# Channel attention feeding a gated MLP: seven-product pairs in batches 0 and 3, other tiles for staging and squares, a changed plan

## The chip, the core and the metric

The kernel runs on one core of one Trainium2 chip. The metric is the device time of one execution, in microseconds (us).

## What is computed

For each of B = 4 batches, with N = 6080 tokens and C = 256 channels, all in float32:

```python
qn = q / (norm(q, over tokens) + 1e-6)          # q, k, v: (4, 6080, 256)
kn = k / (norm(k, over tokens) + 1e-6)
s  = kn.T @ qn / tau                            # 256 x 256 channel scores
a  = exp(s - s.max(-1));  a /= a.sum(-1) + 1e-9
x  = v @ a                                      # 24320 tokens x 256 in all
h  = x @ w_in                                   # 256 -> 2048
g  = h * sigmoid(1.702 * h)
out = g @ w_out                                 # 2048 -> 256
```

The weights come as 64-bit floats and are turned into float32 on the chip.

## The kernel before

**Folding.** The kernel never forms x. For each batch it multiplies a with w_in once (`weights`, matmuls at line 689) and then applies that product to v. Tokens lie last, so a chunk is 1024 tokens wide (the sixth of a batch 960), cut into two halves of 512 (480) columns. A batch has six chunks, and a chunk has eight *pairs* (`NPAIR`), each for 256 of the 2048 hidden features. Pairs are numbered through by `place`: eight in a chunk, 48 in a batch.

**Three matmuls for one product.** A float32 operand is split in a rounded high part and the rest (the helper `cast` at line 283 on ScalarE, `low` at line 306 on VectorE). `three` (line 773) multiplies high by high, high by low and low by high: three matmuls make one *product*.

**Seven or eight products.** A pair multiplies 2 x 2 blocks twice. The first time (`front`: weights w by values v, into the PSUM banks X, Y, Z) it always takes seven products by a Strassen-like scheme. Then ScalarE applies the gate (line 799), and the result is the tile ga, the matrix G of the title. The second time (`back`: G by w_out, into the banks O2, O3, O4, O7 and K) it takes eight plain products, or seven. With seven (`is_s`), VectorE first forms sums of blocks of G in the tile gp (three additions: p13 over 1024 columns, p2 and p4 over 512), and casts and rests are made of the tiles gi (1536 columns), gr and gj (1024 each). With eight, only gi and gj of 1024 columns each are made.

**Groups.** `groups_of(b, c)` says for each chunk how its eight pairs are grouped: a tuple (a, z) is a group of a pairs in seven products followed by z in eight. A group uses the one bank K in turn for the sums of M1, M6, M5 (if a > 0) and of plain products (if z > 0); each sum is taken out of K before the next begins (`evac`, tiles ka to kd; ScalarE copies in a chunk's first group, VectorE adds in later ones). The weights of M6 and M5 of a group are in one tile wb, a slot for each pair of seven. Chunk 0 of batch 0 has two groups (0, 4).

**The attention side.** For batches 0 and 1 the scores are made directly from float32 rows of q and k (`load_direct`, then `unit`, matmuls at line 536); for 2 and 3 from parts that POOL's queue casts while loading (line 280, matmuls at line 542). A unit is two tiles of 128 tokens. Beside the scores it squares the rows (ScalarE, line 512 or 519) and adds the squares to acc (VectorE, line 291); the first matmuls of `finish` (line 588) sum acc over partitions for the norms. `finish` goes on with a power on POOL, scaling, the exponentials (line 628) and a dummy gate that loads the gate's table again (line 640). For batch 0 the squares go to the tile wi, for batch 1 to gp, each a single buffer; raw rows come in four tiles gr0, gj0, gr1, gj1 for batch 0 and in gr0, gr1 for batch 1.

**Conversions.** In chunk 0 of batch 0, w_in and w_out are converted piecewise (`win_convert`, `wout_convert`): loaded as words in the raw tile vr (the same as for the values' v_raw), worked on by VectorE, stored to win_d and wout_d, and loaded from there for use. `wout_convert` works in the tile gr2.

**The order.** Nothing is issued directly. `Plan.add` records each step with its engine, a cost in ns, a lag until its result is there, its dependencies, its tiles and a due time. `Plan.order` places all steps on the engines with a list schedule, forward and backward four times over, and keeps the shortest plan; between engines it counts `HOP` ns. The engines then run their steps in that order. Work for a later batch is tied to a place by `todo`: score units of batch 2 to places 19 to 60, of batch 3 to 74 to 118, softmax and weights after them. Each such step depends, for its loads, on `here`, the first product M1 of the pair at its place.

## Time and profile before

| what | value |
| --- | --- |
| runs | 2161.42, 2163.58, 2167.99 us, median 2163.58 |
| the profiled execution's own time | 2159.93 us |
| its span in the trace | 2158.2 us |
| busy: TensorE matmuls, weight loads | 2107.5 us (98%), 1748.2 us (81%) |
| busy: VectorE, ScalarE, GpSimd | 1831.9 us (85%), 1600.6 us (74%), 77.8 us (4%) |
| granted TensorE clock, mean | 0.993 |
| moved by DMA | 513.24 MB, 238 GB/s |

The page gives for each engine its busy time, then groups of instructions by line, tile and shape, with what ended the idle time before them. PE is TensorE's matmuls, PEld its weight loads, DVE VectorE, ACT ScalarE, POOL GpSimd and SP the engine that issues most DMAs. Matmuls overlap, so the duration of one is not its pitch.

### The profile page before, as it was taken

To read this page: it belongs to the slowest core of one execution; us is meant where nothing else is said; L and a number is where in the kernel's file an instruction comes from. 1 tells how busy PE (TensorE), PEld (TensorE's weight loads), DVE (VectorE), ACT (ScalarE), POOL (GpSimd) and SP (SyncE) were. 2 spreads that over 40 slices of the span, in tenths; PEclk is the share of its full clock that TensorE was granted. 3 is DMA by queue.
4 is the path that set the end of the run, shared out by engine and by line. 5 is a ranking of instruction groups with operands and counts; after the bars stand their busy time and mean duration, and the time that the engine had idled before them with its cause. 6 is when DMAs were issued, how large, how long until landed. Compare 5 with 4: busy or idle time off the path is not lost.

```text
span 2158.2 us, 27036 instructions
## 1 busy us (share of the span) xinstructions
PE 2107.5 (98%) x9724; PEld 1748.2 (81%) x9724; DVE 1831.9 (85%) x2295; ACT 1600.6 (74%) x2345; POOL 77.8 (4%) x110
## 2 busy tenths in 40 slices
PE   8698999999999999999999999999999999999999
PEld 7586788888888888878888888878888888888887
DVE  6897877888878889888898898898987978888796
ACT  4575877676777778877777777787777778777775
POOL 0000000000000000000000000000000000000000
PEclk9899999999999999999999999999999999999999
DMA  8897677767677656886776777647856655655553
GB/s 307 276 327 261 244 278 271 241 227 253 216 250 260 212 207 237 324 263 213 260 251 227 243 250 243 214 168 290 299 195 225 225 190 197 223 195 204 205 200 140
DMA packets 204150, 513.24 MB, mean 238 GB/s; under 512 B 16112, under 2 KB 82160, under 8 KB 202992
## 3 DMA queue, kind: packets, MB, share of 16 engines
q1 hardware_dynamic: 178096, 486.60, 64.0%
q0 software_dynamic: 25920, 24.91, 4.8%
q8 instruction: 77, 1.26, 0.2%
q14 instruction: 57, 0.47, 0.1%
HBM read 444.60 MB, written 66.85 MB: 237 GB/s over the span
## 4 chain that ended last, share of the span: by engine, by line
PE 78%; DVE 9%; DMA 6%; issue 3%; ACT 2%; SPq 0%; POOL 0%; POOLq 0%; DVEq 0%; ACTq 0%
PE ps_o L773 24%; PE ps_X L773 15%; PE ps_k L773 13%; PE ps_Y L773 10%; PE ps_Z L773 10%; PE ps_s L542 3%; PE ps_w L689 2%; DVE acc L291 2%; PE ps_s L536 2%; DMA w<-w_d 1%; DMA v_raw<-in_vT 1%; DMA hl<-in_k 1%; DVE gi L306 1%; DVE gp L291 1%; DMA raw<-in_k 1%
## 5 line engine op out<-in xcount | busy, mean ns | idle before, releaser
L773 PE MATMUL ps_X<-v,w 128*128 128x512 f32 (+1 forms) x1728 | 489.6, 392 | 5.7 <-DVE ga L291 1.7
L773 PE MATMUL ps_o<-gi,wo 128*128 128x512 f32 (+1 forms) x1536 | 412.2, 388 | 0.1
L773 PEld LDWEIGHTS ps_X<-v,w 128*128 128x128 f32 x1728 | 320.4, 188 | 80.2 <-ACT ps_Z L283 7.9
L799 ACT ACTIVATE ga<-ga 128x512 f32<-128x512 f32 (+1 forms) x384 | 237.3, 627 | 184.4 <-DVE ga L291 183.2
L306 DVE TENSOR_TENSOR gi<-ga,gi 128x1536 fp32r<-128x1536 f32 (+2 forms) x192 | 299.8, 1561 | 50.9 <-ACT gi L283 46.1
L773 PE MATMUL ps_Z<-v,w 128*128 128x512 f32 (+1 forms) x1152 | 326.4, 391 | 9.0 <-ACT w L283 5.4
L773 PEld LDWEIGHTS ps_o<-gi,wo 128*128 128x128 f32 x1536 | 287.6, 188 | 58.4 <-DVE gi L306 0.5
L773 PE MATMUL ps_Y<-v,w 128*128 128x512 f32 (+1 forms) x1152 | 326.2, 391 | 0.8 <-DVE ga L291 0.6
L773 PE MATMUL ps_o<-gj,wo 128*128 128x512 f32 (+1 forms) x1152 | 310.0, 390 | 1.2 <-DVE gj L306 1.1
L283 ACT CAST gi<-ga 128x1536 fp32r<-128x1536 f32 (+2 forms) x192 | 254.9, 1328 | 20.2 <-PE ps_o L773 14.6
L773 PEld LDWEIGHTS ps_Z<-v,w 128*128 128x128 f32 x1152 | 215.2, 188 | 58.3 <-ACT w L283 6.1
L773 PEld LDWEIGHTS ps_o<-gj,wo 128*128 128x128 f32 x1152 | 215.8, 189 | 45.2 <-DVE gj L306 1.7
L773 PEld LDWEIGHTS ps_Y<-v,w 128*128 128x128 f32 x1152 | 211.2, 188 | 48.3 <-ACT ps_Y L283 4.5
L773 PE MATMUL ps_k<-gr,wb 128*128 128x512 f32 (+1 forms) x768 | 205.0, 388 | 0.0
L291 DVE TENSOR_TENSOR gp<-ga 128x1024 f32<-128x1024 f32 (+1 forms) x128 | 154.9, 1210 | 35.4 <-ACT ga L799 34.3
L306 DVE TENSOR_TENSOR gj<-gp,gj 128x1024 fp32r<-128x1024 f32 (+1 forms) x128 | 154.7, 1209 | 22.1 <-ACT gj L283 21.8
L291 DVE TENSOR_TENSOR ga<-ps_X,m 128x512 f32<-128x512 f32 (+1 forms) x192 | 130.4, 679 | 49.6 <-PE ps_X L773 40.0
L306 DVE TENSOR_TENSOR gr<-gp,gr 128x1024 fp32r<-128x1024 f32 (+1 forms) x128 | 154.6, 1208 | 17.4 <-ACT gr L283 17.4
L773 PEld LDWEIGHTS ps_k<-gr,wb 128*128 128x128 f32 x768 | 143.4, 188 | 29.4 <-ACT ka L283 0.4
L283 ACT CAST gr<-gp 128x1024 fp32r<-128x1024 f32 (+1 forms) x128 | 133.2, 1041 | 28.7 <-DVE gp L291 23.6
L283 ACT COPY ps_Y<-ps_X 128x512 f32<-128x512 f32 (+1 forms) x192 | 110.7, 577 | 54.1 <-PE ps_X L773 52.7
L291 DVE TENSOR_TENSOR ga<-ps_Y,m 128x512 f32<-128x512 f32 (+1 forms) x192 | 130.4, 679 | 22.3 <-PE ps_Y L773 22.3
(119 smaller groups left out, 2834.6 us busy)
## 6 DMA issues: line engine op xcount, KB each, us to landing
w<-w_d SPq DMA_DIRECT2D x184, 896.0 KB, 5.4
wo<-wout_d SPq DMA_DIRECT2D x128, 640.0 KB, 5.8
wo<-wout_d SPq DMA_DIRECT2D x64, 512.0 KB, 5.7
wb<-wout_d SPq DMA_DIRECT2D x128, 256.0 KB, 3.9
w_d<-wst SPq DMA_DIRECT2D x24, 896.0 KB, 5.2
v_raw<-in_vT SPq DMA_DIRECT2D x20, 1024.0 KB, 8.5
out_T<-oc SPq DMA_DIRECT2D x80, 256.0 KB, 5.2
wi<-win_d SPq DMA_DIRECT2D x32, 512.0 KB, 5.3
```

The costliest lines, as they stand in the source:

```text
L283: return g.add("ACT", act(n, psum), lambda: nc.scalar.copy(dst(), src()), deps, uses, due)
L291: return g.add("DVE", dve(n), lambda: nc.vector.tensor_tensor(dst(), a(), b(), op=op), deps, uses, due)
L306: lambda: nc.vector.tensor_tensor(dst(), src(), hi().bitcast(F32), op=ALU.subtract),
L536: nc.tensor.matmul(out, lhsT=buf()[:pp, 1, o + j, ci], rhs=buf()[:pp, 0, o + j, :], start=begin, stop=True, skip_group_check=True,)
L542: nc.tensor.matmul(out, lhsT=hl()[:pp, 1, j, l, ci], rhs=hl()[:pp, 0, j, r, :], start=begin and m == 0, stop=True, skip_group_check=True,)
L689: nc.tensor.matmul(pb()[:, i * 2 * P : (i + 1) * 2 * P], lhsT=at.aT()[:, l, j, ci], rhs=wi()[:, m, j, :], start=i == 0 and n == 0, stop=Tr ...
L773: nc.tensor.matmul(dst, lhsT=l(a), rhs=r(b), start=begin and n == 0, stop=True, skip_group_check=True,)
L799: lambda: nc.scalar.activation(dst(), src(), AF.Gelu_apprx_sigmoid, scale=sign), deps, uses, at,
```

## The change

Batch 0 gets the groups of batches 1 and 2 in its chunks 1 to 5 (six pairs of eight in seven products, before four of eight). Batch 3 gets groups of three, three and two pairs, all in seven products. Raw rows of batch 1 come in four tiles for the first eight loads, then in two. Batch 0's squares go to the weight tiles w0 and w1 in turn, batch 1's are made in place, after the scores that read the tile; batch 1's acc lies in gp instead of wb. `win_convert` loads its words in gr2 instead of vr, and `wout_convert` works in wb instead of gr2. The exponentials and the dummy gate become separate steps. Loads tied to a place depend on M1 of the pair two places before. The plan counts 70 ns for a hop and longer lags for the score loads.

```diff
-    HOP = 40
+    HOP = 70
...
 ONE, TWO, THREE = ((2, 2), (2, 2)), ((3, 1), (3, 1)), ((3, 0), (3, 0), (2, 0))
...
     if b == c == 0:
         return FIRST
-    return (ONE, TWO, TWO, TWO)[b]
+    return (TWO, TWO, TWO, THREE)[b]
...
+AHEAD = 2
+STAGES = ("gr0", "gj0", "gr1", "gj1") * 2 + ("gr0", "gr1") * 4
...
-        return g.add("POOL", 800, lambda: nc.gpsimd.dma_start(dst(), src()), deps, uses, due, lag=6000)
+        return g.add("POOL", 800, lambda: nc.gpsimd.dma_start(dst(), src()), deps, uses, due, lag=8000)
...
-        f = sbuf("gr2", [P, 8, P], F32, "cf")
+        f = sbuf("wb", [P, 8, P], F32, "cf")
...
-            self.acc = sbuf("wb" if b == 1 else "acc", [P, 2, UT, C], F32, "acc")
+            self.acc = sbuf("gp" if b == 1 else "acc", [P, 2, UT, C], F32, "acc")
...
-                        lambda i=i: view(i), lambda i=i: self.rows(i, t0, nt, pp), 128 * nt, after, [t], due - 10, 5000,
+                        lambda i=i: view(i), lambda i=i: self.rows(i, t0, nt, pp), 128 * nt, after, [t], due - 10, 7000,
...
-                sq = sbuf(("wi", "gp")[self.b], [P, 2, UT, C], F32, "sq") if self.direct else buf
-                s = g.add(
-                    "ACT", act(w),
-                    lambda: nc.scalar.activation(sq()[:pp, :, :nt, :], src(), AF.Square), ok, [buf, sq], due + 1,
-                )
...
+                sq = buf if self.b else sbuf(f"w{u % 2}", [P, 2, UT, C], F32, "sq")
+                sqv = (lambda: src()) if self.b else (lambda: sq()[:pp, :, :nt, :])
+                if self.b == 1:
+                    ok = news
+                s = g.add(
+                    "ACT", act(w),
+                    lambda: nc.scalar.activation(sqv(), src(), AF.Square), ok, [buf, sq], due + 1,
+                )
...
-            e = g.add("ACT", 4200, fn_ee, e, [both, mx, zs], due + 0.9)
+            e = [
+                g.add("ACT", 700 + 1300 * (i == 0), lambda i=i: fn_e(i), [e[i]], [both, mx, zs], due + 0.9 + 0.01 * i)
+                for i in range(NC2)
+            ]
+
+            g.add(
+                "ACT", 1500, lambda: nc.scalar.activation(mx(), mx(), AF.Gelu_apprx_sigmoid), e, [mx], due + 0.95,
+            )
...
-        nxt.load_direct(t0, RT, f"gr{slot % 2}", -80.0 + 2.2 * t0)
+        nxt.load_direct(t0, RT, STAGES[slot], -80.0 + 2.2 * t0)
...
+            heres.append(here)
...
-                    win_convert(grp, cc, t + 3 + 3 * cc, "vr", "oc1")
+                    win_convert(grp, cc, t + 3 + 3 * cc, "gr2", "oc1")
...
-                fn(t, here)
+                fn(t, heres[max(0, place - AHEAD)])
```

The blocks that square and add in `unit` also move behind the scores of the unit, in the order in which steps are recorded.

## Rows read from the trace of the kernel before

**Rows 1.** The page's part 1: busy time, share of the span, instructions.
```profile
PE 2107.5 (98%) x9724; PEld 1748.2 (81%) x9724; DVE 1831.9 (85%) x2295; ACT 1600.6 (74%) x2345; POOL 77.8 (4%) x110
```
**Rows 2.** Stretches: from:to, length, each engine's busy time (instructions), granted clock, DMA.
```profile
0.00:75.00 75.00, 55.07 (x263) 47.62 (x264) 53.15 (x78) 37.57 (x43) 1.73 (x7) 0.90 0.85 298
75.00:197.00 122.00, 116.10 (x539) 97.08 (x538) 110.44 (x179) 83.83 (x120) 0.00 (x0) 0.98 0.82 286
197.00:222.00 25.00, 17.93 (x66) 12.89 (x65) 17.99 (x30) 13.28 (x20) 0.00 (x0) 0.80 0.88 323
300.00:700.00 400.00, 397.43 (x1882) 331.84 (x1881) 329.06 (x394) 288.88 (x429) 30.21 (x42) 1.00 0.74 247
700.00:900.00 200.00, 199.53 (x945) 166.20 (x944) 178.38 (x233) 161.01 (x238) 6.04 (x9) 1.00 0.69 242
900.00:1690.00 790.00, 780.13 (x3619) 646.72 (x3618) 697.25 (x847) 604.57 (x890) 38.85 (x51) 1.00 0.70 239
1690.00:2100.00 410.00, 409.87 (x1798) 334.97 (x1798) 342.64 (x401) 314.22 (x465) 0.00 (x0) 1.00 0.59 204
2100.00:2159.00 59.00, 54.24 (x251) 46.42 (x249) 40.78 (x48) 33.85 (x52) 0.00 (x0) 1.00 0.40 143
```
**Rows 3.** Stretches, the same columns: two of the minutes with the busiest VectorE.
```profile
720.00:780.00 60.00, 59.53 (x277) 48.81 (x276) 57.19 (x69) 47.51 (x68) 3.58 (x6) 1.00 0.66 223
1320.00:1380.00 60.00, 58.77 (x274) 48.52 (x274) 56.46 (x67) 46.10 (x66) 3.96 (x6) 1.00 0.67 222
```
**Rows 4.** TensorE's waits, 60 to 120 us: who <- for what, us, times, longest.
```profile
PE ps_n L588 <- DVE acc L291: 13.3, 1, 13.3
PE ps_s L536 <- DMA raw<-in_k: 5.6, 3, 4.0
```
**Rows 5.** The start in order of time: start, us, engine, instruction [idle before].
```profile
18.70 1.06 ACT L519 ACTIVATE sq<-raw 128x1024 f32<-128x1024 f32 x1 [1.29 <-DVE acc L291]
19.79 1.23 DVE L291 TENSOR_TENSOR acc<-acc,sq 128x1024 f32<-128x1024 f32 x1 [1.12 <-ACT sq L519]
...
56.80 1.03 PE L536 MATMUL ps_s<-raw 128*128 128x256 f32 x4
...
71.09 1.84 PE L588 MATMUL ps_n<-ones,acc 128*128 128x1 f32 x8 [13.27 <-DVE acc L291]
```
**Rows 6.** TensorE's waits, 120 to 330 us: the longest line.
```profile
PE ps_Z L773 <- ACT w L283: 5.4, 2, 4.1
```
**Rows 7.** SP's queue in order of time: the load of chunk 1's values.
```profile
201.85 0.38 SPq L276 DMA_DIRECT2D v_raw<-in_vT  x1
```
**Rows 8.** Groups by shape, whole span: count, busy us, mean ns, idle before.
```profile
L306 DVE TENSOR_TENSOR gi<-ga,gi 128x1536 fp32r<-128x1536 f32 x106 | 185.8, 1753 | 30.8 <-ACT gi L283 26.0 <-PE ps_k L773 4.1
L291 DVE TENSOR_TENSOR gp<-ga 128x1024 f32<-128x1024 f32 x106 | 129.5, 1221 | 27.7 <-ACT ga L799 26.9
L306 DVE TENSOR_TENSOR gj<-gp,gj 128x1024 fp32r<-128x1024 f32 x106 | 129.3, 1220 | 17.3 <-ACT gj L283 17.0
L306 DVE TENSOR_TENSOR gr<-gp,gr 128x1024 fp32r<-128x1024 f32 x106 | 129.2, 1219 | 13.2 <-ACT gr L283 13.2
L291 DVE TENSOR_TENSOR gp<-ga,gp 128x512 f32<-128x512 f32 x106 | 72.7, 686 | 4.0 <-ACT ga L799 1.5
...
L297 DVE SCALAR_TENSOR_TENSOR gj<-ga,gj 128x1024 fp32r<-128x1024 f32 x54 | 66.0, 1222 | 21.5 <-ACT gj L858 21.4
L306 DVE TENSOR_TENSOR gi<-ga,gi 128x1024 fp32r<-128x1024 f32 x54 | 66.0, 1221 | 8.2 <-ACT gi L283 8.1
```
**Rows 9.** VectorE in batch 3 in order of time: two neighbours that overlap.
```profile
1805.21 1.75 DVE L306 TENSOR_TENSOR gi<-ga,gi 128x1536 fp32r<-128x1536 f32 x1
1806.88 1.22 DVE L306 TENSOR_TENSOR gj<-gp,gj 128x1024 fp32r<-128x1024 f32 x1
```
**Rows 10.** VectorE at the end in order of time: K's third sum.
```profile
2149.72 0.66 DVE L291 TENSOR_TENSOR kc<-ps_k,kc 128x480 f32<-128x480 f32 x1 [2.88 <-PE ps_k L773]
```
**Rows 11.** ScalarE in the first softmax in order of time: the table load.
```profile
82.69 1.28 ACT L640 ACT_TABLE_LOAD   x1
```

More of the change, by code (lines that the diff above doesn't have):

```diff
@@ L509, in unit @@
                 ok, uses = [l], [hl]
-            if u == 0:
-                self.acc_n = [g.add(
-                    "ACT", act(w), lambda: nc.scalar.activation(acc(), src(), AF.Square), ok, [buf, acc], due + 0.5,
-                )]
-            else:
-                sq = sbuf(("wi", "gp")[self.b], [P, 2, UT, C], F32, "sq") if self.direct else buf
-                s = g.add(
-                    "ACT", act(w),
-                    lambda: nc.scalar.activation(sq()[:pp, :, :nt, :], src(), AF.Square), ok, [buf, sq], due + 1,
-                )
-                a = lambda: acc()[:pp, :, :nt, :]
-                self.acc_n = [tt(
-                    a, a, lambda: sq()[:pp, :, :nt, :], ALU.add, w, [s, *self.acc_n], [sq, acc], due + 1.5,
-                )]
             S = self.S if self.direct else bank("Z", "s")
@@ L552, in unit @@
                 news.append(n)
+            if u == 0:
+                self.acc_n = [g.add(
+                    "ACT", act(w), lambda: nc.scalar.activation(acc(), src(), AF.Square), ok, [buf, acc], due + 0.5,
+                )]
+            else:
+                sq = buf if self.b else sbuf(f"w{u % 2}", [P, 2, UT, C], F32, "sq")
[6 more added lines that the diff above has]
+                )
+                a = lambda: acc()[:pp, :, :nt, :]
+                self.acc_n = [tt(
+                    a, a, sqv, ALU.add, w, [s, *self.acc_n], [sq, acc], due + 1.5,
+                )]
             if self.direct:
@@ L635, in finish @@
             ]
-            def fn_ee():
-                for i in range(NC2):
-                    fn_e(i)
-                nc.scalar.activation(mx(), mx(), AF.Gelu_apprx_sigmoid)
-            e = g.add("ACT", 4200, fn_ee, e, [both, mx, zs], due + 0.9)
+            e = [
[5 more added lines that the diff above has]
+            )
             def fn_z():
@@ L648, in fn_z @@
                     nc.vector.tensor_scalar_mul(x()[:, i, :], x()[:, i, :], zs()[:, i : i + 1])
-            e = g.add("DVE", 1300, fn_z, [e], [both, zs], due + 1)
+            e = g.add("DVE", 1300, fn_z, e, [both, zs], due + 1)
             due = yield
@@ L1094, in channel_attention_then_glu @@
     place = 0
+    heres = []
     for b in range(B):
```

## Prediction

> **What bounds the kernel now.** I read the busy shares first: TensorE is busy for 2107.5 of 2158.2 us [rows 1], so 50.7 us of idle time are all that a better order can win; the rest has to come from less work. Then the table of stretches [rows 2], which splits these 50.7 us: the first 75 us hold 19.9 of them, 75 to 197 us 5.9, the 25 us from 197 on 7.1, the last 59 us under 5. In batch 0 (300 to 700 us) TensorE is idle for 2.6 of 400 us, in batches 1 and 2 (900 to 1690) for 9.9 of 790, in batch 3 (1690 to 2100) for 0.13 of 410. So the start is bound by latency and the steady part by TensorE. VectorE is second: 82% busy in batch 0, 88% in batches 1 and 2, 84% in batch 3. Two dense minutes show what follows above that: at 95% and 94% VectorE, TensorE still ran for 99.2% and 98.0% of the time [rows 3]. Last I read what TensorE waits for in the start [rows 4, 6] and the instructions there in order of time [rows 5, 7].
>
> **Fewer products.** A pair of seven products issues 42 matmuls, one of eight 45. Batch 3's stretch has 409.87 us for 1798 matmuls, 0.228 us each [rows 2]. A product of three is then 0.684 us, and in the sixth chunk (480 instead of 512 columns) 480/512 of it, 0.641. Batch 0 changes two pairs in each of chunks 1 to 5: 8 x 0.684 + 2 x 0.641 = 6.8 us less. Batch 3 changes two in each of six: 10 x 0.684 + 2 x 0.641 = 8.1 us. Together 14.9 us, all where TensorE is full.
>
> **What they cost VectorE.** A pair of seven has six instructions there in place of two: 1.753 + 1.221 + 1.220 + 1.219 + 2 x 0.686 = 6.8 us against 1.222 + 1.221 = 2.4 [rows 8]. Independent neighbours start some 0.08 us before the other's end (1805.21 + 1.75 is past 1806.88) [rows 9], so four more instructions give back 0.3: 4.0 us a pair, 8.0 a chunk. ScalarE, 77% busy in batch 3 [rows 2], gets one more cast a pair and stays off the limit. Batch 3 also gets a third group with three partial sums: nine evacuations instead of eight, six instead of four of them on VectorE, 2 x 0.6 more: 9.2 us a chunk.
> Batch 3: a chunk is 342 x 0.228 = 78.0 us now, VectorE's share of it 342.64/409.87, 65.2 us. After: 336 x 0.228 = 76.6 us for TensorE and 74.4 for VectorE, 97%, above every stretch of [rows 2, 3]. Bounds: TensorE stays full (nothing lost), or VectorE only reaches the 89% that it held over 200 us beside a full TensorE [rows 2]; then a chunk takes 74.4/0.892 = 83.4 us. I take 1.5% of idle TensorE, between the 0.8% and 2.0% of [rows 3], the rows nearest to it: 6.9 us of 456. With 1 us for the tail (below) batch 3 comes out even, -8.1 + 6.9 + 1 = 0, with bounds of -8 and +33.
> Batch 0 becomes what batches 1 and 2 are now: six pairs of eight in seven products, with another batch's scores between them. There TensorE idles 1.25%, here 0.64%. Five chunks are about 430 us (348 x 0.228 each, and the scores): 2.6 us more idle time, so net -4, bounds -7 (none) and +2 (2%, as the denser minute of [rows 3]).
>
> A rule of the notes speaks against the whole edit. In [rows 2] batch 3 has weight loads 82% busy and VectorE 84%, while matmuls are at 100%. The Trainium skill (Perfetto Trace Analysis, Identifying the Most-Contended Engine) holds matmul busy time for a poor measure, wants weight-load busy time or achieved FLOPs in its place, and has the engine with the highest share relieved first. By that VectorE is the bound already, six matmuls fewer are worth nothing and VectorE's work costs in full (rival one). The trace does not agree: VectorE leaves 67 of these 410 us unused, TensorE 0.13.
>
> **The tail.** The last pair becomes one of seven, whose VectorE chain is longer, with K's three sums behind it. Before, VectorE waited 2.88 us for K's third sum of the last group [rows 10], while O products filled TensorE. One more dependent sum costs 0 (O products still fill it) to 4 us (nothing does). I take 1, since the last pair has four O products to put there.
>
> **The start.** Squares and additions alternate on one tile: a square of 1.06, an addition of 1.23, and 1.29 of waiting before the next square [rows 5]. 24 units at 2.35 us with conversions among them end at 71 us; TensorE's scores end at 57.8, and it waits 13.3 us for the sum [rows 4, 5]. The change lets batch 0's squares alternate between the two weight tiles, not needed before the first weights, so additions can follow each other at 1.23 - 0.08 = 1.15 us: 24 x 1.15 = 28 us from 10 us on. With the first conversions among them they could end soon after the scores, and the stages of raw rows come free sooner. Batch 1's rows get four stages instead of two for their first eight loads, so that TensorE has scores to do while the softmax chain runs; now it waits 5.6 us for such loads [rows 4]. Their squares are done in place and now wait for the scores that read the tile; behind them on ScalarE stand gates and casts of the first pairs, which TensorE's next products need.
> Second, the conversions of w_in and w_out share one raw tile with the values, which for chunk 1 load only at 201.85 [rows 7]; the weights of the last pairs come late as well. TensorE waits 5.4 us for them [rows 6] and needs 17.93 us for 66 matmuls at a granted clock of 0.80, a mix of 1.2 and 2.4 GHz [rows 2]. The change gives w_in's words a tile of their own, so the two kinds of load overlap.
> Upper end: 13.3 + 5.6 + 7.1 of idle time and some 4 for matmuls at 1.2 GHz, 30 us. VectorE sets about the same end: it has 53.2 + 110.4 + 18.0 = 181.6 us of work up to 222 us [rows 2], from 10 us on. Lower end: -5 (a loss), if pairs 0 and 1, whose gj tiles are now stages, wait for batch 1's sums, which stand behind conversions on VectorE. It is 90% busy from 75 to 197 us, so an earlier start is partly taken back. I take 13, the wait with the plainest cause.
>
> The exponentials and the table load for the gates become three instructions. The normalisation no longer waits for the load of 1.28 us [rows 11], in the first batch on the path; it is inside the 13. But another pair's gate may now come between two exponentials, and two loads more with it, 2.6 us. The Trainium skill (ScalarE: Activation LUTs, Table sets: the hidden batching unit) asks for the opposite, all calls of one set together. By its 2.66 us a switch (same page, What ACT_TABLE_LOAD costs) two switches in the start would make the sum 5.3 us worse, an estimate. A row shows 1.28 of each; the drain in that figure stands in none.
>
> **Order.** A longer hop in the plan (70 for 40 ns), later arrivals for loads, and score loads that may go two pairs sooner change the order of every queue, SP's and POOL's too, where these loads pass loads of weights. Bounds: most of the 9.9 us of batches 1 and 2 gone (-8), or as much again (+10). I take -2.
>
> **Sum.** -13 - 4 + 0 - 2 = -19. The profiled execution took 2159.93 us, 1.7 more than its span, and would take 2141. The median of the runs shown, 2163.58, lies 3.65 higher; by it I forecast 2163.6 - 19 = 2145.
>
> **Rivals.**
> One, slower: VectorE takes over as the bound of batch 3. For it: 97% is beyond anything seen, the one gp tile carries its chain in every pair, and no pair of eight is left to catch up in. Against it: at 95% TensorE kept 99.2%. It decides from there on. At 83.4 us a chunk batch 3 costs 5 x 5.4 + 5 + 1 = 33 us instead of 0: 2145 + 33 = 2178.
> Two: the start gains nothing, since VectorE's queue there is full and the first pairs wait for their gj. 2145 + 13 = 2158.
> Three: all saved products are kept, and 20 us of the start's gaps close. -6.8 - 8.1 + 1 - 20 - 2 = -36, 2128.
> Four: each part does its work, but the new order is worse where nothing else changed, +10 for -2: 2157.
>
> **Chances.** Forecast 0.47 (own range 2137 to 2153), one 0.11, two 0.17, three 0.17, four 0.08. A measurement of this kernel tells about 0.3%, 6.5 us, from no change; that is 2157. Faster: 0.47 + 0.17 + 0.06 of two + 0.04 of four = 0.74; same: 0.11 + 0.04 + 0.02 of one = 0.17; slower: 0.09. The range of 8 in 10 runs from below rival three to beyond rival two: 2125 to 2163.
>
> **What would show it.** Batch 3: 36 matmuls fewer, VectorE near 97%, TensorE idle for some 7 us; if VectorE binds, its own waits vanish and TensorE's name gi, gj, gr or ga. Start: the norm's matmuls wait under 4 us, the gap near 200 us is closed, the first outputs leave some 13 us sooner. I am wrong if they leave no sooner, or if a chunk of batch 3 takes over 78 us.

## The result, and the profile after

The changed kernel takes 2117.77 us (median of four runs, 2116.12 to 2118.23), the one before 2164.58 us in the same comparison: a ratio of 0.9782, 95% interval 0.9765 to 0.9799, or 47 us less. 2145 was forecast, and the range began at 2125: the direction was right, but the forecast gain of 19 us is less than half of the measured one. The profiled execution took 2116.12 us, its span is 2114.4. Of all runs below one, of the kernel with only the exponentials in one step, took 2966.84 us at a granted clock of 0.65; it is left out.

The page's busy line of the changed kernel, which answers [rows 1]:

```profile
PE 2082.2 (98%) x9658; PEld 1737.6 (82%) x9658; DVE 1918.6 (91%) x2395; ACT 1620.3 (77%) x2361; POOL 76.7 (4%) x110
```

66 matmuls fewer, TensorE's idle time down from 50.7 to 32.2 us, VectorE up by 87 us. Stretches of the changed kernel, with the columns of [rows 2]:

```profile
0.00:75.00 75.00, 62.11 (x283) 53.94 (x284) 61.26 (x97) 40.13 (x48) 1.83 (x7) 0.89 0.96 348
75.00:153.00 78.00, 76.05 (x368) 63.73 (x366) 74.95 (x123) 60.15 (x85) 0.00 (x0) 1.00 0.95 342
153.00:197.00 44.00, 43.70 (x208) 36.25 (x208) 38.33 (x63) 32.33 (x50) 0.00 (x0) 1.00 0.75 266
197.00:222.00 25.00, 24.92 (x118) 20.37 (x116) 18.71 (x38) 19.64 (x33) 1.01 (x1) 1.00 0.60 217
...
1650.00:2056.00 406.00, 405.80 (x1784) 333.00 (x1783) 391.11 (x455) 325.24 (x472) 0.00 (x0) 1.00 0.62 218
2056.00:2115.00 59.00, 50.80 (x233) 43.03 (x231) 46.76 (x55) 36.02 (x52) 0.00 (x0) 0.97 0.40 144
```

The gap near 200 us is gone: TensorE works 24.92 of 25 us at a granted clock of 1.00, where it was 17.93 at 0.80. In batch 3 VectorE is busy 96.3% of the time and TensorE still 405.80 of 406 us. The first 153 us now move 342 to 348 GB/s with the DMA engines 95 to 96% busy.

To say where the 43.8 us between the two spans went, I cut both traces at the same places: where the first product of a chunk's first pair begins (in time that is M5, with M1 behind it; pair 0; pair 8, chunk 1; pairs 48, 96, 144, the first of batches 1, 2, 3). Stretches cut so, same columns, the kernel before:

```profile
0.00:99.30 99.30, 74.41 (x348) 63.89 (x349) 74.37 (x117) 52.36 (x64) 1.73 (x7) 0.90 0.83 286
99.30:224.88 125.58, 117.57 (x532) 95.87 (x531) 108.38 (x171) 84.94 (x124) 0.00 (x0) 0.96 0.83 295
224.88:660.21 435.33, 431.97 (x2054) 360.84 (x2053) 354.83 (x444) 321.06 (x478) 28.36 (x39) 1.00 0.73 245
660.21:1177.43 517.22, 511.61 (x2406) 425.28 (x2404) 461.60 (x566) 399.89 (x585) 28.99 (x41) 1.00 0.73 249
1177.43:1673.99 496.56, 491.84 (x2273) 407.44 (x2273) 433.44 (x534) 381.01 (x562) 18.77 (x23) 1.00 0.69 235
1673.99:2158.20 484.21, 480.12 (x2119) 394.88 (x2117) 399.29 (x469) 361.34 (x536) 0.00 (x0) 1.00 0.56 197
```

and the changed kernel:

```profile
0.00:98.40 98.40, 83.68 (x388) 72.31 (x389) 84.14 (x141) 59.22 (x72) 1.83 (x7) 0.91 0.95 340
98.40:202.60 104.20, 103.78 (x495) 86.25 (x494) 94.62 (x148) 77.13 (x116) 0.00 (x0) 1.00 0.86 315
202.60:634.04 431.44, 426.71 (x2030) 356.69 (x2029) 390.47 (x480) 332.88 (x488) 28.36 (x39) 1.00 0.76 257
634.04:1142.37 508.33, 505.42 (x2390) 423.90 (x2389) 461.13 (x566) 394.27 (x582) 30.03 (x41) 1.00 0.74 250
1142.37:1636.20 493.83, 492.25 (x2286) 410.76 (x2285) 438.16 (x540) 384.29 (x567) 16.43 (x23) 1.00 0.69 238
1636.20:2114.40 478.20, 470.40 (x2077) 387.67 (x2075) 450.08 (x525) 372.55 (x541) 0.00 (x0) 1.00 0.59 209
```

| stretch | before, us | after, us | difference | forecast |
| --- | --- | --- | --- | --- |
| up to chunk 1 | 224.9 | 202.6 | -22.3 | -13 |
| rest of batch 0 | 435.3 | 431.4 | -3.9 | -4 |
| batches 1 and 2 | 1013.8 | 1002.2 | -11.6 | -2 |
| batch 3 and the end | 484.2 | 478.2 | -6.0 | 0 |

The forecast of -2 is the prediction's term for the order, set against the batches from which its bounds were taken. Batches 1 and 2, whose groups did not change, issue 3 matmuls fewer in all (2406 + 2273 against 2390 + 2286), some 0.7 us: of the other 11 us, 5.8 are idle time of TensorE (10.3 before, 4.5 after) and some 5 are busy time, matmuls that took less long. In batch 3, 42 matmuls fewer at 0.228 us are 9.6 us; 3.6 of them are lost again, at the end (below).

What TensorE waits for from 60 to 120 us (answers [rows 4]), and two loads on SP's queue (chunk 1's values, 201.85 in [rows 7]; the first outputs, at 241.15 in the trace of before):

```profile
PE ps_n L593 <- DVE acc L293: 8.8, 1, 8.8
PE ps_s L523 <- DMA raw<-in_k: 1.5, 2, 1.3
```

```profile
177.19 0.38 SPq L278 DMA_DIRECT2D v_raw<-in_vT  x1
212.62 0.34 SPq L278 DMA_DIRECT2D out_T<-oc  x1
```

The norm's wait fell only from 13.3 to 8.8 us, and pair 0 begins only 0.9 us sooner. The first outputs leave 28.5 us sooner. So the start's gain does not lie where the forecast put it; nearly all of it lies between pair 0 and chunk 1.

### The profile page after: what moved, and what is told of

It reads as the page before. It is cut to its first block, busy times and chain, and to the rows that moved or that the text cites. A ratio compares the mean times of both kernels' runs of the same rounds, so it can differ in the third digit from the quotient of the medians.

```text
span 2114.4 us, 27101 instructions
## 1 busy us (share of the span) xinstructions
PE 2082.2 (98%) x9658; PEld 1737.6 (82%) x9658; DVE 1918.6 (91%) x2395; ACT 1620.3 (77%) x2361; POOL 76.7 (4%) x110
## 4 chain that ended last, share of the span: by engine, by line
PE 80%; DVE 9%; DMA 6%; ACT 3%; issue 1%; SPq 1%; POOL 0%; DVEq 0%; ACTq 0%
PE ps_o L780 23%; PE ps_X L780 16%; PE ps_k L780 14%; PE ps_Y L780 11%; PE ps_Z L780 10%; PE ps_s L529 3%; PE ps_w L696 2%; DMA hl<-in_k 2%; DVE gp L293 1%; PE ps_s L523 1%; DVE gi L308 1%; DMA out_T<-oc 1%; DVE ga L293 1%; DMA v_raw<-in_vT 1%; DVE acc L293 1%
## 5 line engine op out<-in xcount | busy, mean ns | idle before, releaser
L780 PE MATMUL ps_o<-gi,wo 128*128 128x512 f32 (+1 forms) x1404 | 375.7, 388 | 1.3 <-DVE gi L308 1.3
L308 DVE TENSOR_TENSOR gi<-ga,gi 128x1536 fp32r<-128x1536 f32 (+2 forms) x192 | 311.1, 1621 | 27.4 <-ACT gi L285 26.6
L780 PEld LDWEIGHTS ps_o<-gi,wo 128*128 128x128 f32 x1404 | 262.7, 188 | 54.5 <-DVE gi L308 1.6
L780 PE MATMUL ps_k<-gr,wb 128*128 128x512 f32 (+1 forms) x900 | 239.6, 388 | 0.0
L308 DVE TENSOR_TENSOR gr<-gp,gr 128x1024 fp32r<-128x1024 f32 (+1 forms) x150 | 181.0, 1207 | 23.2 <-ACT gr L285 23.2
L293 DVE TENSOR_TENSOR gp<-ga 128x1024 f32<-128x1024 f32 (+1 forms) x150 | 181.4, 1209 | 21.1 <-ACT ga L806 18.1
L780 PEld LDWEIGHTS ps_k<-gr,wb 128*128 128x128 f32 x900 | 168.3, 188 | 34.0 <-DVE kb L293 0.3
L308 DVE TENSOR_TENSOR gj<-gp,gj 128x1024 fp32r<-128x1024 f32 (+1 forms) x150 | 181.0, 1206 | 9.9 <-ACT gj L285 9.8
L285 ACT CAST gr<-gp 128x1024 fp32r<-128x1024 f32 (+1 forms) x150 | 156.2, 1042 | 43.9 <-DVE gp L293 33.4
L285 ACT CAST gj<-gp 128x1024 fp32r<-128x1024 f32 (+1 forms) x150 | 156.2, 1041 | 8.4 <-DVE gp L293 7.4
L293 DVE TENSOR_TENSOR ga<-ps_Y,m 128x512 f32<-128x512 f32 (+1 forms) x192 | 130.4, 679 | 25.9 <-PE ps_Y L780 25.4
```

What stands on the lines that cost most here:

```text
L285: return g.add("ACT", act(n, psum), lambda: nc.scalar.copy(dst(), src()), deps, uses, due)
L293: return g.add("DVE", dve(n), lambda: nc.vector.tensor_tensor(dst(), a(), b(), op=op), deps, uses, due)
L308: lambda: nc.vector.tensor_tensor(dst(), src(), hi().bitcast(F32), op=ALU.subtract),
L780: nc.tensor.matmul(dst, lhsT=l(a), rhs=r(b), start=begin and n == 0, stop=True, skip_group_check=True,)
```

## The experiments

A kernel's start is judged by when chunk 1 begins (202.6 us in the changed kernel, 224.9 before), the rest by the lengths of the stretches above. Differences in time are between medians. Three words name the parts: *groups* (the numbers of pairs in seven products), *tiles* (stages, squares, raw tiles, and the split exponentials with them), *plan* (hop, lags, AHEAD). A diff is against the changed kernel where the kernel before is not named, and `...` stands for lines left out.

**Groups alone**, on the kernel before.

```diff
-    return (ONE, TWO, TWO, TWO)[b]
+    return (TWO, TWO, TWO, THREE)[b]
```

> The kernel before with the new groups alone (six pairs of eight in seven products in batch 0, all eight in batch 3). Theory A, the parts add up: the changed kernel gained 14.9 us of products less 4.9 us of added stalls in batches 0 and 3, so this one should take 2164.6 - 10 = 2154.6 us, with the start as before and 66 matmuls fewer. Theory B, the seven-product pairs only pay with the new tiles and plan, because VectorE at 96% needs them: 2164 us or more, with TensorE stalls of 10 us or more in batch 3. My own step on record (1.5% of idle TensorE in batch 3): 2160.

2164.94 us, ratio 1.0003 (0.9993 to 1.0013). All 15 us of products are gone from TensorE's work and none from the time: the rest of batch 0 takes 437.4 us for 435.3, batch 1 519.7 for 517.2, and chunk 1 begins at 229.5 instead of 224.9. Groups on the old tiles and plan are worth nothing.

**All but the groups.**

```diff
-    return (TWO, TWO, TWO, THREE)[b]
+    return (ONE, TWO, TWO, TWO)[b]
```

> The changed kernel with the old groups: tiles, staging and plan alone. Theory A, parts add up: 2117.8 + 10 = 2127.8 us; the start as in the changed kernel (chunk 1's first pair at about 203 us instead of 225) and the stalls of batches 1 and 2 halved. Theory B, the groups gain only together with the rest: 2117.8 + 15 to 20, so 2133 to 2138.

2124.38 us (0.9806 to 0.9835). With new tiles and plan, the groups are worth 6.6 us of their 15. Most of the 47 us is elsewhere.

**The old plan.**

```diff
-    HOP = 70
+    HOP = 40
...
-AHEAD = 2
+AHEAD = 0
...
-        return g.add("POOL", 800, lambda: nc.gpsimd.dma_start(dst(), src()), deps, uses, due, lag=8000)
+        return g.add("POOL", 800, lambda: nc.gpsimd.dma_start(dst(), src()), deps, uses, due, lag=6000)
...
-                        lambda i=i: view(i), lambda i=i: self.rows(i, t0, nt, pp), 128 * nt, after, [t], due - 10, 7000,
+                        lambda i=i: view(i), lambda i=i: self.rows(i, t0, nt, pp), 128 * nt, after, [t], due - 10, 5000,
```

> The changed kernel with the plan's old numbers: hop 40, lags 6000 and 5000, loads tied to the pair at their own place. Theory A: these numbers are what halved TensorE's stalls in batches 1 and 2 (21.9 to 10.9 us), so 2117.8 + 11 = 2129 us, stalls of about 22 us in batches 1 and 2, start nearly as in the changed kernel. Theory B: the stalls fell because another tile assignment gave another plan, not because of these numbers: 2118, within 3 us.

2150.27 us (0.9914 to 0.9953): the plan's four numbers, put at -2 in the prediction, are worth 32 us here. (The traced execution is one of 2142.56 us, so the stretches show some 26 of them.) The start keeps all it won, chunk 1 begins at 198.0. The loss comes after: batch 0's rest 441.0 us for 431.4, batch 1 520.5 for 508.3, batch 2 500.0 for 493.8. TensorE's waits in this kernel from 203 to 2060 us:

```profile
PE ps_k L780 <- DVE gi L308: 5.5, 6, 1.6
PE ps_s L529 <- DVE hl L308: 5.0, 7, 0.9
PE ps_s L529 <- DMA hl<-in_k: 3.1, 2, 2.2
```

In the changed kernel the second of these is 1.2 us and the third 0.8, and the first does not appear.

**One number at a time.** The hop:

```diff
-    HOP = 70
+    HOP = 40
```

> The changed kernel with the hop at 40 ns alone. With all three old numbers the kernel took 2150 us (2142.6 when profiled), and its stalls after chunk 0 were 61 us instead of 32. Theory A, the hop did it: a plan that counts a handoff 30 ns too short puts TensorE's next product up to the wait itself, many small stalls; 2140 to 2150. Theory B, loads did it (lags and the place they are tied to): within 4 us of 2118.

2116.3 us (0.9764 to 0.9803): nothing. The place to which loads are tied, with the long lags kept:

```diff
-AHEAD = 2
+AHEAD = 0
```

> The changed kernel with loads tied to the pair at their own place again, alone. Theory A (hop): 2118 to 2122. Theory B (loads): the late loads of scores and of weights show as waits of TensorE for hl and w, 2128 to 2145.

2200.63 us, ratio 1.0169 (1.0152 to 1.0187): 83 us more, and slower than the kernel before. Batches 0 to 2 take 458.6, 542.7 and 516.3 us; batch 3, without scores of a later batch, 478.5 as in the changed kernel. From the start of chunk 1 to that of batch 3 TensorE issues as many matmuls as in the changed kernel. The two stretches, first this kernel, then the changed one:

```profile
199.65:1717.34 1517.69, 1453.70 (x6704) 1184.84 (x6703) 1294.45 (x1584) 1117.96 (x1635) 76.12 (x103) 1.00 0.69 234
```

```profile
202.60:1636.20 1433.60, 1424.38 (x6704) 1191.36 (x6703) 1289.75 (x1584) 1111.44 (x1635) 74.82 (x103) 1.00 0.73 248
```

So TensorE's idle time rises from 9.2 to 64.0 us, and its busy time by 29.3. Its three longest waits from 203 to 1650 us in this kernel:

```profile
PE ps_s L529 <- DVE hl L308: 17.6, 15, 2.5
PE ps_k L780 <- DVE gi L308: 10.8, 17, 1.2
PE ps_X L780 <- ACT ps_Z L285: 10.2, 17, 1.3
```

The two lags, changed as in the old plan, with AHEAD kept:

```diff
-        return g.add("POOL", 800, lambda: nc.gpsimd.dma_start(dst(), src()), deps, uses, due, lag=8000)
+        return g.add("POOL", 800, lambda: nc.gpsimd.dma_start(dst(), src()), deps, uses, due, lag=6000)
...
```

> The changed kernel with the old lags of the score loads (6000 and 5000) alone. Theory A (hop): 2118 to 2121. Theory B (loads): VectorE's subtraction for the scores waits on landing loads and holds its queue, 2123 to 2140.

2128.2 us (0.9818 to 0.9856), 10 more. Here it is VectorE that waits, standing at a subtraction whose data hasn't landed. Its waits from 203 to 1650 us, first this kernel, then the changed one:

```profile
DVE hl L308 <- issue: 25.3, 12, 3.9
```

```profile
DVE hl L308 <- issue: 5.7, 4, 2.6
```

The row names no load, but in this kernel's trace each of the 12 waits ends within 0.2 us of the landing of hl's load (hl from k), which takes 6.5 us as a median from its issue, longer than the lag of 6000 ns.

Four places instead of two:

```diff
-AHEAD = 2
+AHEAD = 4
```

> The changed kernel with loads tied to the pair four places before instead of two. Theory: two places already put the score subtraction some 5 us ahead of the scores, so nothing is left to win: 2118 us (2114 to 2122). Rival one: more slack wins again, since TensorE still waits some us before scores; 2105 to 2112. Rival two: loads that stand earlier hold the raw tiles longer and pass the loads of weights; 2124 or more.

2117.96 us (0.977 to 0.98): no more to win.

In these traces I measured each of the 50 score units of batches 2 and 3, as medians. With AHEAD 0 (the kernel before, groups alone, tiles alone, the old plan, AHEAD 0 with long lags) the subtraction ends 0.2 to 0.6 us before the unit's first score matmul; with AHEAD 2 or 4 it ends 3.4 to 7.2 us before it. The loads are not what is late with AHEAD 0. Those of hl are issued in every kernel 0.3 us after the last scores of the unit before, which used the same tile, and the subtraction begins 17 to 19 us after the first of them with AHEAD 0 and 8 to 10 us with AHEAD 2 or 4. Its data, raw rows included, has by then lain ready for 7.0 us with AHEAD 0 and long lags, for 4.8 with the old plan, for 3.1 in the changed kernel and for 1.1 with the old lags. So the tie and the lag act on where the planned order puts the subtraction: too late, and TensorE stands before the scores; too early, and VectorE stands at the load.

TensorE's gaps right before these scores sum to 17.8 us with AHEAD 0 and long lags, 8.1 with the old plan, 2.3 in the changed kernel, 2.3 with tiles alone, 3.8 with groups alone and 2.7 in the kernel before. They are a part only of what the plan is worth: 5.8 of the 32 us between the old plan and the changed kernel, 15.5 of the 83 with long lags. The rest is spread over many waits, most of them for VectorE and ScalarE, and over busy time; which step of the order makes each of these is not shown. The cell between, old lags with AHEAD 0, was run only with hop 40 as well.

**The new plan on the kernel before**: HOP = 70, the long lags, and loads tied two places earlier.

```diff
+            heres.append(here)
...
-                fn(t, here)
+                fn(t, heres[max(0, place - 2)])
```

> The kernel before with the three new numbers of the plan alone: old tiles, old groups. Stalls after chunk 0 were 33 us there, of which 25 in batches 0 to 2. Theory A, the numbers help any plan of this kernel: they halve that, 2164 - 12 = 2152, with the start as before. Theory B, they matter only where VectorE is over 90% busy (the new groups): 2160 to 2166.

2153.77 us over ten runs (0.9945 to 0.9975), so -9; chunk 1 begins at 229.6. (The traced execution is the longest of the ten, 2161.13 us.)

**Tiles alone; groups and plan without tiles.** These complete the table of eight. First the changed kernel with the old plan and, beside it, the old groups:

```diff
-    return (TWO, TWO, TWO, THREE)[b]
+    return (ONE, TWO, TWO, TWO)[b]
```

> The changed kernel with the groups and the plan's numbers of the kernel before: only tiles, stages, squares and split exponentials are new. Theory of this study: the start's gain of some 22 us stands by itself, so the second chunk begins near 200 us as with the old plan and the new groups (198.0), while the steady part idles as before: 2163 - 22 = 2141 us (2136 to 2148). Rival: tiles and plan only work together, since earlier pairs meet score loads that come too late; then the start's gain is given back later on and the time is 2152 to 2160.

2141.36 us (0.9885 to 0.9918); chunk 1 begins at 200.5. Then the kernel before with the new plan and, beside it, the new groups:

```diff
-    return (ONE, TWO, TWO, TWO)[b]
+    return (TWO, TWO, TWO, THREE)[b]
```

> The kernel before with the new groups and the new plan's numbers, without the new tiles. Theory: the new plan keeps what the groups save, because the score subtractions are placed well before the scores in a busier VectorE; then it gains what the groups are worth on the new tiles (6.6 us) on the plan alone (2153.8), 2147 us (2142 to 2151). Rival: the groups' products are lost again to VectorE without the new tiles, as with the old plan, and the time stays at 2154 (2152 to 2158).

2142.99 us (0.9891 to 0.9921); chunk 1 begins at 227.7.

| medians, us | old plan, old groups | old plan, new groups | new plan, old groups | new plan, new groups |
| --- | --- | --- | --- | --- |
| old tiles | 2163 | 2164.9 | 2153.8 | 2143.0 |
| new tiles | 2141.4 | 2150.3 | 2124.4 | 2117.8 |

The tiles gain in every column (22, 15, 29, 25 us). On the old plan the groups cost 9 us with the new tiles, and with the old ones the difference of 2 is inside the noise (the interval of its ratio holds 1); on the new plan they gain 11 and 7. The plan is worth 9 and 17 us with old groups, 22 and 32 with new. The three parts alone add up to 22 - 2 + 9 = 29 us; together they give 45. Most of the difference lies between groups and plan (groups do better by 13 us on the new plan than on the old with old tiles, by 16 with new ones); tiles do 8 us better with the new plan and 7 worse with the new groups, which cancels. A reading that fits is that seven-product pairs load VectorE, and that TensorE pays for it where the order leaves no slack. The waits bear it out in part only: with groups alone the gaps before scores are 1.1 us longer than in the kernel before, and the products saved are 15 us.

**Parts of the tiles.** Batch 0's squares on one weight tile; two stages for batch 1; the words of w_in in vr again:

```diff
-                sq = buf if self.b else sbuf(f"w{u % 2}", [P, 2, UT, C], F32, "sq")
+                sq = buf if self.b else sbuf("w0", [P, 2, UT, C], F32, "sq")
```

> The changed kernel with batch 0's squares on one tile (w0) instead of two in turn. Theory A, my step on record (the squares' chain makes the start): the norm's matmuls come back to 71 us from 65.6 and TensorE waits 13 us again, chunk 1 starts 8 to 13 us later, 2126 to 2131 in all. Theory B, the conversions make the start: 2117 to 2121, chunk 1 at 203 to 206 us.

2124.66 us (0.9811 to 0.984), 7 more; chunk 1 begins at 208.8.

```diff
-STAGES = ("gr0", "gj0", "gr1", "gj1") * 2 + ("gr0", "gr1") * 4
+STAGES = ("gr0", "gr1") * 6
```

> The changed kernel with batch 1's rows in two tiles (gr0, gr1) as before. By the ledger of the two traces, 40 matmuls of batch 1's scores (8.6 us) moved from chunk 0 to the time before pair 0, which the four tiles allow. Theory A: they come back into chunk 0, 2117.8 + 6 to 9 = 2124 to 2127. Theory B, other work fills the time before pair 0 as well: 2117 to 2121.

2122.69 us (0.9796 to 0.9829), 5 more; chunk 1 begins at 208.5. The norm's matmuls in order of time:

```profile
54.06 1.02 PE L593 MATMUL ps_n<-ones,acc 128*128 128x1 f32 x8 [1.43 <-DVE acc L293]
```

They wait 1.43 us, not 8.8, and pair 0 begins at 83.1, 15 us sooner than in the changed kernel. Yet chunk 1 begins 6 us later. With hop 40, whose tiles are all those of the changed kernel, the norm's matmuls come at 54.87 without a wait, pair 0 at 85.6, and chunk 1 at 202.0 as in the changed kernel. So the norm's wait does not set the start's end: what TensorE has not done of batch 1's scores before pair 0 it does after it (of 384 score matmuls 240 come before pair 0 here, 300 in the changed kernel), and the loads and conversions for the first pairs are no earlier.

```diff
-                    win_convert(grp, cc, t + 3 + 3 * cc, "gr2", "oc1")
+                    win_convert(grp, cc, t + 3 + 3 * cc, "vr", "oc1")
```

> The changed kernel with w_in's words in vr again, the tile they shared with w_out's and with the values. Theory A (squares make the start): within 4 us of 2118. Theory B (conversions make it): the last weights of chunk 0 come late again, TensorE idles 7 us near 190 us and runs some 10 us at 1.2 GHz: 2117.8 + 12 = 2130, chunk 1 at about 215 us.

2136.53 us (0.987 to 0.9899), 19 more; chunk 1 begins at 219.4. Two stretches of this kernel, then TensorE's waits from 84 to 222 us:

```profile
153.00:197.00 44.00, 30.04 (x126) 22.63 (x126) 30.89 (x54) 20.84 (x31) 0.00 (x0) 0.89 0.63 224
197.00:222.00 25.00, 21.77 (x82) 16.09 (x81) 16.81 (x27) 16.00 (x26) 0.42 (x1) 0.79 0.73 268
```

```profile
PE ps_w L696 <- DMA wi<-win_d: 5.8, 1, 5.8
PE ps_Z L780 <- ACT w L285: 5.4, 3, 3.5
```

This is the gap of before ([rows 6], 5.4 us for w, clock 0.80), back in its place: pair 0 still begins early (85.7 us), and then the conversions come late, TensorE does 126 matmuls in 44 us instead of 208, and the DMA engines are 63% busy. What the start follows is the last of these conversions. The load of the last weights for chunk 0 on SP's queue, in the kernel before, in the changed one and in this one:

```profile
198.98 0.33 SPq L276 DMA_DIRECT2D wi<-win_d  x1
```

```profile
176.71 0.32 SPq L278 DMA_DIRECT2D wi<-win_d  x1
```

```profile
192.94 0.33 SPq L278 DMA_DIRECT2D wi<-win_d  x1
```

Chunk 1 begins 25.9, 25.9 and 26.4 us later, and in all 20 kernels of this document 24.0 to 27.2 us later, though this load lies anywhere from 171.2 to 205.6 us and pair 0 anywhere from 83 to 105. So the chain of conversions of w_in, slowed by the raw tile that it shares, bounds the start, and not the bandwidth.

The other two are less sure. In the kernels with all new tiles chunk 1 begins anywhere from 196.5 to 205.8 us, although none of them touches the start's tiles: any edit gives another order. 208.8 and 208.5 lie only 3 us beyond that. Batch 1's squares in place, its acc in gp and the tile wb in `wout_convert` were not undone by themselves.

**Exponentials and dummy gate in one step again; only the exponentials in one step.**

```diff
-            e = [
-                g.add("ACT", 700 + 1300 * (i == 0), lambda i=i: fn_e(i), [e[i]], [both, mx, zs], due + 0.9 + 0.01 * i)
-                for i in range(NC2)
-            ]
-            g.add(
-                "ACT", 1500, lambda: nc.scalar.activation(mx(), mx(), AF.Gelu_apprx_sigmoid), e, [mx], due + 0.95,
-            )
+            def fn_ee():
+                for i in range(NC2):
+                    fn_e(i)
+                nc.scalar.activation(mx(), mx(), AF.Gelu_apprx_sigmoid)
+            e = [g.add("ACT", 4200, fn_ee, e, [both, mx, zs], due + 0.9)]
```

> The changed kernel with the two exponentials and the dummy gate as one step again. Theory: a separate dummy gate lets the normalisation start one table load (1.28 us) sooner, on the path only in the first batch: 1 to 3 us slower than with the split (2119 to 2121). Rival: with the split another pair's gate comes between exponentials and loads the table twice more, so that one step is better: 2113 to 2116.

2110.68 us (0.9746 to 0.9775): 7 less than with the split.

```diff
-            e = [
-                g.add("ACT", 700 + 1300 * (i == 0), lambda i=i: fn_e(i), [e[i]], [both, mx, zs], due + 0.9 + 0.01 * i)
-                for i in range(NC2)
-            ]
+            def fn_ee():
+                for i in range(NC2):
+                    fn_e(i)
+            e = [g.add("ACT", 2700, fn_ee, e, [both, mx, zs], due + 0.9)]
```

> The changed kernel with the two exponentials in one step and only the dummy gate apart. Theory one, the split exponentials cost: in the first softmax two squares stand between them, 3.2 us from one to the next where they follow each other at 0.5 when fused; then this version loses that and comes near 2111 us (2109 to 2114). Theory two, the dummy gate apart costs, since it is issued late or other gates load the table: 2118 us (2115 to 2121). Theory three, neither matters by itself and the order of the start changes by chance with any edit of the list of steps: pair 0 starts anywhere from 90 to 100 us and the time lies anywhere from 2108 to 2120, without a row in the softmax that explains it.

2111.24 us over three runs (0.9737 to 0.9778). So the kernels without the split are some 6 us faster, and the dummy gate by itself makes no difference. ScalarE in the first softmax in order of time, the changed kernel and then the last one:

```profile
77.41 0.51 ACT L633 ACTIVATE x<-x,mx 128x256 f32<-128x256 f32 x1 [0.17 <-DVE mx L630]
...
77.92 1.04 ACT L552 ACTIVATE raw<-raw 128x1024 f32<-128x1024 f32 x1
79.64 1.06 ACT L552 ACTIVATE raw<-raw 128x1024 f32<-128x1024 f32 x1 [0.67 <-PE ps_s L523]
80.60 0.49 ACT L633 ACTIVATE x<-x,mx 128x256 f32<-128x256 f32 x1
```

```profile
70.14 0.50 ACT L633 ACTIVATE x<-x,mx 128x256 f32<-128x256 f32 x1
...
70.99 0.51 ACT L633 ACTIVATE x<-x,mx 128x256 f32<-128x256 f32 x1 [0.25 <-DVE mx L630]
```

With the split, two of batch 1's squares stand between the exponentials: 3.19 us from one to the next instead of 0.85. That makes the first softmax 2.3 us longer, but that this reaches the end is not shown, since chunk 1 does not follow pair 0. In the last kernel the start is 6.1 us shorter, and there the load of the last weights comes at 171.2 instead of 176.7, which no row ties to the split; in the one before it 3.5 us lie in the start and 3.6 in the rest of batch 0. Whether the 6 us are the split or an order that happened to be better stays open. A gate between the exponentials, with two more table loads, is not it: there are eight table loads in the trace before, eight in the changed kernel's and eight with one step.

**Where VectorE does become the bound.** Batch 1 in groups of three too:

```diff
-    return (TWO, TWO, TWO, THREE)[b]
+    return (TWO, THREE, TWO, THREE)[b]
```

> The changed kernel with all eight pairs in seven products in batch 1 as well, where the scores of batch 3 run beside them. VectorE has 461 us in batch 1's 508; with 9.2 us more a chunk it would need 516 us of the 500 that TensorE needs, 103%. Theory A, VectorE costs nothing up to about 97% and then sets the pace: batch 1 takes 516 to 530 us, in all 2126 to 2140. Theory B, VectorE still has hidden room (its busy time counts waits) or the plan moves its work out of the batch: 2117.8 - 8 = 2110.

2115.95 us (0.9763 to 0.9796), the same time. Batch 1 of this kernel as a stretch:

```profile
628.69:1143.74 515.05, 506.49 (x2381) 422.93 (x2380) 506.97 (x626) 410.97 (x589) 30.02 (x41) 1.00 0.75 257
```

VectorE is busy 506.97 of 515.05 us, 98.4%, and the batch takes 6.7 us longer than in the changed kernel although 12 pairs have a product less (8.1 us, as for batch 3 in the prediction). Batches 1 and 2 together take 1006.4 us for 1002.2, so all that the products save is given back, and more. VectorE's own work, 507 us, is more than the some 500 (508.3 - 8.1) that TensorE would need. By name TensorE's 8.6 us of idle time there end with loads of weights from w_d (5.0 us) more than with VectorE (2.4 us), so that VectorE binds is read from its busy time and not from these waits. Nor does it bind everywhere above 96%: in the batch's first chunk, with scores of batch 2 between, TensorE loses nothing beside a VectorE that is busy for 99.3% of the time.

```profile
628.69:713.43 84.74, 84.74 (x403) 71.28 (x402) 84.11 (x100) 67.90 (x98) 6.83 (x10) 1.00 0.72 239
```

The whole comes out even only since chunk 1 happens to begin 3.9 us sooner here, at 198.7.

**Groups of three in two more chunks, and the best of all.**

```diff
-    return (TWO, TWO, TWO, THREE)[b]
+    return THREE if b == 2 and c >= 4 else (TWO, TWO, TWO, THREE)[b]
```

> The changed kernel with all eight pairs in seven products in chunks 4 and 5 of batch 2 too, where no scores run any more. Four products fewer, 2.7 us; VectorE has 86% of TensorE's time there, so after it 98%. If VectorE costs nothing up to 98%: 2115. If it sets the pace above 97%: 2118 to 2121.

2114.78 us (0.9768 to 0.9798), 3 less, inside the interval of the changed kernel. These two chunks carry no scores of another batch, like batch 3. With the exponentials and the dummy gate in one step as above, beside these groups:

```diff
-            e = [
...
+            e = [g.add("ACT", 4200, fn_ee, e, [both, mx, zs], due + 0.9)]
```

> Exponentials and dummy gate as one step again and groups of three, three, two in the last two chunks of batch 2. If the two gains add up (7.1 and 3.0 us), 2108 us (2105 to 2110); if the second is only order, 2111 (2109 to 2114).

2106.85 us, ratio 0.9736 (0.9721 to 0.975): 11 us less than the changed kernel, where the two gains by themselves, 7.1 and 3.0, add up to 10.

## Why the prediction was right in direction and too small

Three terms of the sum failed, and each was too small. The order stood at -2, and batches 1 and 2 gave -11.6. The start stood at -13 and gave -22.3, by another cause than the one priced. Batch 3 stood at 0 and gave -6.0, since the price of 6.9 us for VectorE did not come. By parts taken back out of the changed kernel, the groups, priced at -4, are worth -6.6; the tiles, priced at -13, -25; and the plan, priced at -2, -32. So the step that failed most is the price of the order: it was read from TensorE's idle time in the kernel before, as if the order were a part by itself.

**Fewer products: right in number.** 66 matmuls fewer, 15 us by 0.228 each, against 14.9. What they are worth in time depends on the plan, which no term of the sum held.

**VectorE's load: right, and its price in batch 3 wrong.** It rose by 50.8 us in the last stretch, 8.5 a chunk (9.2 forecast), and stands at 96.3% (97% forecast). But the 1.5% of idle TensorE, 6.9 us, did not come: 0.2 of 406 us. The step that failed took the price from [rows 3], minutes in which scores of another batch share the queues. Batch 3 has none. In batch 1, which has them, the price is there once its groups are changed too (98.4%, the product savings lost). That the scores make the difference is not shown: batch 1's first chunk has them and lost nothing at 99.3%. So rival one describes a real bound, in the wrong batch. Of the Trainium skill's rule (Perfetto Trace Analysis, Identifying the Most-Contended Engine), by which matmul busy time is a poor measure and VectorE or the weight loads would have been the bound already, the trace of after shows the contrary in batch 3: six matmuls fewer a chunk were worth their full time up to the tail with VectorE at 96%. That busy time can hide waits is true here as well: the same 6704 matmuls were busy for 1424.4 us in the changed kernel and for 1453.7 with AHEAD 0.

**The tail: 1 us forecast, 3 measured.** The ends of the two kernels in order of time, before and after:

```profile
2152.78 1.46 PE L773 MATMUL ps_o<-gi,wo 128*128 128x480 f32 x6
2154.28 0.66 DVE L291 TENSOR_TENSOR oc<-ps_o,kb 128x480 f32<-128x480 f32 x1 [0.47 <-PE ps_o L773]
```

```profile
2106.70 0.81 PE L780 MATMUL ps_o<-gj,wo 128*128 128x480 f32 x3
2106.89 0.66 DVE L293 TENSOR_TENSOR kc<-ps_k,kc 128x480 f32<-128x480 f32 x1 [0.79 <-PE ps_k L780]
2107.59 1.22 DVE L299 SCALAR_TENSOR_TENSOR oc<-ps_o,kc 128x480 f32<-128x480 f32 x2
2110.38 0.66 DVE L293 TENSOR_TENSOR oc<-ps_o,kb 128x480 f32<-128x480 f32 x1 [1.57 <-DMA out_T<-oc]
```

TensorE ends 3.9 us before the span before (2158.2 - 2154.24) and 6.9 after (2114.4 - 2107.51). The last K sum feeds two outputs, and the chunk's last output then waits 1.57 us for oc, still being stored. That wait was not seen; the O products were no cover, as they ran out at the same time. With it, batch 3 is -9.6 + 3 + 0.6 for scattered idle = -6.

**Batch 0: right**, -3.9 for -4, but only with the new plan; with the old one its rest got longer (437.4 and 441.0 us).

**The start: inside its bounds, sum too small, cause wrong.** -22.3 for -13. I took the norm's 13.3 us, "the wait with the plainest cause". It still stands at 8.8, where under 4 was expected, and where it was gone (two stages, hop 40) chunk 1 came no sooner. The additions do follow each other without a wait for squares, as forecast; but pieces of conversions now stand between them. VectorE in the changed kernel's start in order of time, which answers [rows 5]:

```profile
16.21 1.22 DVE L293 TENSOR_TENSOR acc<-acc,sq 128x1024 f32<-128x1024 f32 x1
17.34 0.42 DVE L374 TENSOR_SCALAR low<-cv 128x512 uint32<-128x512 uint32 x1
17.68 1.22 DVE L293 TENSOR_TENSOR acc<-acc,sq 128x1024 f32<-128x1024 f32 x1
18.82 0.42 DVE L353 TENSOR_SCALAR cf<-cf 128x512 f32<-128x512 f32 x1
```

So idle time of VectorE went to conversions (it is busy for 84.1 us up to pair 0, 74.4 before). What carried the gain is what the prediction named second, the raw tile of their own (19 us when undone): the load of chunk 0's last weights comes 22.3 us sooner, and chunk 1 with it.

**Exponentials: wrong sign.** Counted as a small gain inside the start, the split went with a loss of some 6 us here. The prediction set the Trainium skill's advice beside it (ScalarE: Activation LUTs, Table sets: the hidden batching unit: keep the calls of one table set together), with an estimate of 5.3 us for two more loads. The size comes near, but the trace does not show that reason, since no load was added.

**Order: the term that was most mis-sized**, -2 with bounds of -8 and +10, where undoing it costs 32 us. The bound failed since it was taken from the idle time of batches 1 and 2 before, 9.9 us: that is what an order could win at the old load. What an order is worth once another part loads VectorE more was not in any row of before. And batches 1 and 2 alone gave 11.6, beyond the bound, as busy time held waits too: some 5 us of it with nearly as many matmuls. This is also where rival three fell short: it kept the products and closed 20 us of the start, but kept -2 for the order.

## What to carry to other kernels

- Parts of a change that load the same engine, or take load off it, can't be priced one by one: products saved at the price of VectorE work were worth nothing or a loss of 9 us on one plan and 7 to 11 us on another. Ask of each cost what slack it falls on, and of each change of order what it makes possible.
- In a list-scheduled kernel, look where the plan puts the work on a load: behind the landing and some us before its use. Here that took an earlier tie and lags that cover the landing, and either half alone was worse than both (10 and 83 us).
- In a latency-bound start, the longest wait need not be the bound: find the step that the end follows in several versions, here the load of the last weights, and look for a buffer that serializes the longest chain of loads, here one raw tile for two kinds of load, and see whether the DMA engines have room.

## What was not expected of the hardware

TensorE lost 0.2 of 406 us beside a VectorE busy for 96.3% of them and nothing of 84.74 at 99.3%, but 8.6 of the 515 us of that whole batch, at 98.4%. So VectorE's share alone does not tell what TensorE loses. And the granted clock followed the gaps: in the 25 us from 197 on it was 0.80 where TensorE was idle for 7.1 of them (before) and 0.79 where it had been idle for 14 of the 44 us ahead (one raw tile), a mix of its two levels of 1.2 and 2.4 GHz; it was 1.00, all at 2.4 GHz, where TensorE had been busy for 43.70 of those 44.
